# Softmax normalising on GpSimd before MLP 1, and another order and other buffers where MLP 2 follows MLP 1

## The chip, the core and the metric

One core of a Trainium2 chip runs the whole program once. The metric is the device time in microseconds (us), median of several executions. A profile of one execution gives, for each engine, every instruction with its start and its duration. Engines: PE (TensorE: matrix products, with PEld for its weight loads), DVE (VectorE), ACT (ScalarE), POOL (GpSimd) and SP (SyncE, which here issues all DMAs).

## What is computed

Windowed attention with four sink columns, then two two-layer MLPs, all in float32 at the outside:

```python
scores = where(is_sink | in_window, q @ k.T / sqrt(64), -1e9)     # 2 x 8 heads, 768 x 768, window 128
a = exp(scores - max); a = a / (a.sum(-1) + 1e-9)
x = (a @ v) -> 1536 tokens x 512
h = x @ w1_in;  g = h * clip(h + 3, 0, 6) / 6;            y = g @ w1_out      # 512 -> 2048 -> 512
h = y @ w2_in;  g = max(h, 0) + log1p(exp(-abs(h)));    out = g @ w2_out      # 512 -> 2048 -> 512
```

The kernel gets the weights as 64-bit floats. Each chunk of 128 columns or rows (512 KB) has to be turned into a high and a low part that the PE takes.

## The kernel before

**Products in three passes.** Each MLP product is three matmuls of 128x512 (high x high, high x low, low x high). An MLP step is one hidden chunk m (of 16) for one block b of 512 tokens (of 3): twelve matmuls into `h`, an activation, and twelve matmuls that add the chunk into the output (`y` in MLP 1, `o` in MLP 2).

**Attention** goes in 48 turns n of 128 queries and two heads. `e_S` makes the scores, `at_exp` (L354, L358) the masked exponentials and their sums, `at_N` (L363) normalises them, `e_T` (L433) and `e_Ts` (L447) transpose them, `e_V` multiplies by v, two turns behind. In `at_N`, L367 and L368 make the reciprocal of the sums on DVE, L371 gathers the normalised sink columns `Ps` on DVE (128x64), and L376 to L379 scale the two heads' `Pt` in place (128x288 each): head 1 on ACT, head 0 on DVE. Turns 0 to 15 come ahead of MLP 1; the other 32 are woven into MLP 1's matmuls by a list (`line`) with due times counted in matmuls.

**Weights.** `w_load` brings a chunk into one of 32 places over the SP queue; `w_conv` (L512) converts it: L28, L29, L32 on DVE, L31 and a copy on ACT (`w<-wraw`, L256), and the subtraction for the low part on POOL (`w<-wraw,w`, L253). `w_step(n)` converts up to n loaded chunks in queue order. `stand` notes a DVE instruction, and for MLP 1's chunks (`gated`, L510) the conversion's DVE instructions are put behind the last but one that was noted. A place comes free (`w_free`) when the last block's step of that chunk has read it.

**MLP 1** runs 48 steps and two more (`for s`, L785): at step s, `m1_h` and `m1_g` of step s and `m1_y` of step s - 2. Activations go through pools `rp` (tile `r`, two buffers) and `gp` (tile `G`, two). During the last block (s from 32) each step appends one or two chunks of MLP 2 to `w2` and loads one; `w_step(2)` converts. The two last steps (s = 48, 49) run `m2_h`, MLP 2's first two products. Then `st_m1` closes `rp`, `gp` and the PSUM pools, and `open_left` opens on the left side `e2` (tiles `ab`, `l`, `d`), `ps_h3` and `ps_o`.

**MLP 2** (`for s`, L821) does at step s `m2_h`, `m2_e` (ACT: L736 to L738), `m2_g` of step s - 1 (DVE L745, L747, L748; POOL `d<-ab,d`, L253; ACT and DVE for G) and `m2_o` of step s - 5. `G2` has three buffers, `h2` in PSUM three and one more.

**Order.** Score, attention and MLP 1 matmuls and the first loads stay in program order. Everything else is ordered for each engine by the framework's scheduler, by program order as priority and by when it takes its inputs to be there. Each engine then runs its queue strictly in order: an instruction that waits holds all behind it.

Of the kernel before, what the change touches and what calls it, by code (L numbers as in the profile page):

```python
# [8 lines left out]
F32 = mybir.dt.float32  # L9
BF16 = mybir.dt.bfloat16  # L10
F32R = mybir.dt.float32r
I32 = mybir.dt.int32
AF = mybir.ActivationFunctionType
ALU = mybir.AluOpType
# [4 lines left out]
SK = 32  # L19
# [158 lines left out]
def window_attention_hardswish_softplus(  # L178
# [17 lines left out]
    nc = tc.nc  # L196
# [3 lines left out]
    P = 128  # L200
    NP = H // 2
    KD = DM // P
    KF = DFF // P
# [9 lines left out]
    left = "left"  # L213
# [4 lines left out]

    TH, TS = (6, 9), 15

    NPP, NRP, NWX = 4, 2, 2

    WL0, WS0 = 1, 14

# [1 line left out]
    right = "right"  # L226
# [16 lines left out]
    T2 = 512  # L243
# [5 lines left out]
    def f32(ap):  # L249
        return ap.bitcast(F32)  # L250

    def sub(eng, out_, a, b):
        return eng.tensor_tensor(out=out_, in0=a, in1=b, op=ALU.subtract)  # L253

    def acopy(out_, in_, scale_=1.0):
        nc.scalar.activation(out=out_, in_=in_, func=AF.Copy, scale=scale_)  # L256
# [70 lines left out]
    A, M, L, pools = {}, {}, {}, {}  # L327
# [11 lines left out]
    def cols(n):  # L339
        k, i = divmod(n, 2)  # L340
        g, p, b, ib = blk(k)
        t = 2 * ib + i
        if t == 0:
            return t, 0, SK + P + SK
        if ib == 0:
            return t, SK, 2 * P + SK
        return t, i * (P + SK), 2 * P + SK
# [15 lines left out]
    def at_N(n):  # L363
        t, c0, w = cols(n)
        Pt = A["P", n]
        sm = A.pop(("sum", n))
        nc.vector.tensor_scalar(sm, sm, 1e-9, None, op0=ALU.add)  # L367
        nc.vector.reciprocal(sm, sm)  # L368
        cs = 0 if t == 0 else P
        Ps = AT["ep"].tile([P, 2, SK], F32, name="Ps", tag="Ps")  # L370
        nc.vector.tensor_tensor(out=Ps, in0=Pt[:, :, cs:cs + SK], in1=sm[:, :, None].to_broadcast([P, 2, SK]),  # L371
                                op=ALU.mult)
        A["Ps", n] = Ps

        for h in range(2):
            if h == 1 or (4 * NP <= n < 8 * NP and n % 2 == 1):  # L376
                acopy(Pt[:, h, :w], Pt[:, h, :w], sm[:, h:h + 1])
            else:
                i = nc.vector.tensor_scalar(Pt[:, h, :w], Pt[:, h, :w], sm[:, h:h + 1], None, op0=ALU.mult)  # L379
                if n < 4 * NP:  # L380
                    stand(i)

# [104 lines left out]
    wq = []  # L489
# [6 lines left out]
    def w_load(kind, m):  # L496
        tag = places.pop(0)
        w = wp.tile([P, 512, 2], I32, name="wraw", tag=tag)
        (load if kind[0] == "1" else nc.sync.dma_start)(
            w.rearrange("p (k f) t -> p k (f t)", k=KD), weight_source(kind[1], m, srcs_w[kind], P, KD))  # L500
        W["raw", kind, m] = w, tag

    after = []

    def stand(ins):
        after.append(ins.ins)
        del after[:-2]

    def gated(kind):
        return len(after) == 2 and kind[0] == "1"  # L510

    def w_conv(kind, m):  # L512

# [21 lines left out]
    def w_step(n=1):  # L535
        for _ in range(n):
            if wq and ("raw",) + wq[0] in W:
                w_conv(*wq.pop(0))
# [28 lines left out]
    def m1_g(b, m):  # L567
        r = M.pop(("r", b, m))
        G = L["gp"].tile([P, 2, T2], F32R, name="G", tag="G")
        acopy(G[:, 0], r)  # L570
        stand(sub(nc.vector, G[:, 1], r, f32(G[:, 0])))
        M["G", b, m] = G

    def m1_y(b, m):
        G = M.pop(("G", b, m))
        if m == 0:
            M["y", b] = [L["ps_y"].tile([P, T2], F32, name=f"y{d}", tag=f"y{d}") for d in range(KD)]
        w = W["1o", m]
        for d in range(KD):
            for j, (a, e) in enumerate(PASSES):  # L580
                mm(out=M["y", b][d], lhsT=w[:, a, d * P:(d + 1) * P], rhs=G[:, e, :],
                   start=(m == 0 and j == 0), stop=(m == KF - 1 and j == 2))
# [19 lines left out]
    L1, L2 = 2, 5  # L602
# [34 lines left out]
    seq = [(b, m) for b in range(NB2) for m in range(KF)]  # L637
    wq = [(kd, m) for m in range(KF) for kd in ("1i", "1o")]
# [2 lines left out]

    KE = 2 * NP
    st_m1 = ExitStack()
    L["rp"] = st_m1.enter_context(tc.tile_pool(name="rp", bufs=NRP, side=left))
    L["ps_h"] = st_m1.enter_context(tc.tile_pool(name="ps_h", bufs=NH, space=PSUM, side=left))
    st_at = e_open()
    st_ps = e_banks(4, 3)
# [35 lines left out]
            w_step()  # L683
    st_ps.close()

    L["gp"] = st_m1.enter_context(tc.tile_pool(name="gp", bufs=2, side=left))
    L["ps_y"] = st_m1.enter_context(tc.tile_pool(name="ps_y", bufs=1, space=PSUM, side=left))
    st_ps = e_banks(NS, NTV)

    n2, n3 = n1 + 4 * NP, n1 + 8 * NP  # L690
# [5 lines left out]
    seq2 = [(b, m) for b in (0, 2, 1) for m in range(KF)]  # L696
    st_m2 = ExitStack()

    def open_right():
        pools["yr"] = st_m2.enter_context(tc.tile_pool(name="yr", bufs=1, side=right))  # L700
        pools["g2"] = st_m2.enter_context(tc.tile_pool(name="g2", bufs=3, side=right))
        pools["ps_h2"] = st_m2.enter_context(tc.tile_pool(name="ps_h2", bufs=NS + NTV, space=PSUM, side=right))

    def open_left():
        pools["e2"] = st_m2.enter_context(tc.tile_pool(name="e2", bufs=2, side=left))
        pools["ps_h3"] = st_m2.enter_context(tc.tile_pool(name="ps_h3", bufs=NH, space=PSUM, side=left))
        pools["ps_o"] = st_m2.enter_context(tc.tile_pool(name="ps_o", bufs=1, space=PSUM, side=left))

# [12 lines left out]
    def m2_h(b, m):  # L721
        w_ready("2i", m)
        Y = M["Y", b]
        hp = pools["ps_h3" if m % 4 < NH and "ps_h3" in pools else "ps_h2"].tile([P, T2], F32, name="h2", tag="h2")
        w = W["2i", m].rearrange("p a (k f) -> p a k f", k=KD)
        for kk in range(KD):
            for j, (a, e) in enumerate(PASSES):
                nc.tensor.matmul(out=hp, lhsT=w[:, a, kk, :], rhs=Y[:, kk, e, :],  # L728
                                 start=(kk == 0 and j == 0), stop=(kk == KD - 1 and j == 2))
        M["h2", b, m] = hp  # L730

    def m2_e(b, m):
        hp = M["h2", b, m]
        ab = pools["e2"].tile([P, T2], F32, name="ab", tag="ab")
        l = pools["e2"].tile([P, T2], F32, name="l", tag="l")
        nc.scalar.activation(out=ab, in_=hp, func=AF.Abs)  # L736
        nc.scalar.activation(out=ab, in_=ab, func=AF.Exp, scale=-1.0)
        nc.scalar.activation(out=l, in_=ab, func=AF.Ln, bias=1.0, scale=1.0)  # L738
        M["e2", b, m] = (ab, l)

    def m2_g(b, m):
        hp, (ab, l) = M.pop(("h2", b, m)), M.pop(("e2", b, m))
        G = pools["g2"].tile([P, 2, T2], F32R, name="G2", tag="G2")
        d = pools["e2"].tile([P, T2], F32, name="d", tag="d")
        nc.vector.tensor_scalar(d, ab, 1.0, -1.0, op0=ALU.add, op1=ALU.add)  # L745
        sub(nc.gpsimd, d, ab, d)
        nc.vector.scalar_tensor_tensor(out=l, in0=hp, scalar=0.0, in1=l, op0=ALU.max, op1=ALU.add)  # L747
        nc.vector.tensor_tensor(out=l, in0=l, in1=d, op=ALU.add)  # L748
        acopy(G[:, 0], l)
        stand(sub(nc.vector, G[:, 1], l, f32(G[:, 0])))  # L750
        M["G2", b, m] = G
# [22 lines left out]
                nc.sync.dma_start(out=dst, in_=o)  # L774

    opened = False
    w2 = []

    def w2_load(n):
        for kind_m in w2[:n]:  # L780
            wq.append(kind_m)
            w_load(*kind_m)
        del w2[:n]

    for s in range(len(seq) + L1):  # L785
        cur = seq[s] if s < len(seq) else None
        prev = seq[s - L1] if s >= L1 else None
        for _ in range(2):
            if wl:
                w_load(*wl.pop(0))  # L790
        if cur:
            w_ready("1i", cur[1])
            m1_h(*cur)
        else:
            m2_h(0, s - len(seq))
        if cur:
            m1_g(*cur)
        if prev:
            w_ready("1o", prev[1])
            m1_y(*prev)  # L800
            if prev[1] == KF - 1:
                m1_yout(prev[0])
        w_step(2)
        if not line and not opened:
            opened = True
            st_ps.close()
            st_at.close()
            open_right()
            at_flag()
            y_load(0)  # L810
        for kind, bm in (("2i", cur), ("2o", prev)):
            if bm and bm[0] == NB2 - 1:
                w2.append((kind, bm[1]))
                w_free("1" + kind[1], bm[1])
        w2_load(1)
    w2_load(len(w2))
    assert opened
    st_m1.close()
    open_left()

    for s in range(len(seq2) + L2):  # L821
        if s < len(seq2):
            b, m = seq2[s]
            if s == 4:
                y_load(1)
            if s >= L1:
                m2_h(b, m)
            m2_e(b, m)
        if 1 <= s <= len(seq2):
            m2_g(*seq2[s - 1])  # L830
        w_step()
        if s >= L2:
            m2_o(*seq2[s - L2])
        w_step()
    st_m2.close()
    st_fin.close()


# [62 lines left out]
```

## Time and profile before

| | |
|---|---|
| median of 3 runs | 695.05 us (694.83 to 695.4) |
| profiled execution: device time, span | 694.55 us, 692.8 us |
| PE busy | 656.7 us, 95% |
| DVE, ACT, POOL busy | 421.7, 381.9, 151.2 us |
| granted TensorE clock, mean | 0.981 |

A busy time is the sum of an engine's instructions. A wait is the idle time of an engine ahead of an instruction, with what ended it in brackets. PE busy time is modelled: its matmuls overlap, so a step's length is better read from the starts of its groups.

### The profile page before, as it was taken

To read this page: it belongs to the slowest core of one execution; us is meant where nothing else is said; L and a number is where in the kernel's file an instruction comes from. 1 tells how busy PE (TensorE), PEld (TensorE's weight loads), DVE (VectorE), ACT (ScalarE), POOL (GpSimd) and SP (SyncE) were. 2 spreads that over 40 slices of the span, in tenths; PEclk is the share of its full clock that TensorE was granted. 3 is DMA by queue.
4 is the path that set the end of the run, shared out by engine and by line. 5 is a ranking of instruction groups with operands and counts; after the bars stand their busy time and mean duration, and the time that the engine had idled before them with its cause. 6 is when DMAs were issued, how large, how long until landed. Compare 5 with 4: busy or idle time off the path is not lost.

```text
span 692.8 us, 9020 instructions
## 1 busy us (share of the span) xinstructions
PE 656.7 (95%) x3151; PEld 493.7 (71%) x3151; DVE 421.7 (61%) x931; ACT 381.9 (55%) x783; POOL 151.2 (22%) x116
## 2 busy tenths in 40 slices
PE   7879899999999999999999996999999999999996
PEld 4446566666676777778787774888888888888884
DVE  4798988887444443425688888954445444454441
ACT  4898777776444554434545667654445444444441
POOL 0013333333000000000244444442222222222220
PEclk8998999999999999999999998999999999999999
DMA  6999652111112100004855541000001000010001
GB/s 186 258 268 294 202 164 86 32 30 48 35 50 80 40 29 16 1 12 146 267 187 180 179 145 38 1 0 1 0 1 61 0 1 1 1 61 0 1 0 66
DMA packets 39541, 54.93 MB, mean 79 GB/s; under 512 B 3136, under 2 KB 29504, under 8 KB 39232
## 3 DMA queue, kind: packets, MB, share of 16 engines
q1 hardware_dynamic: 39488, 54.28, 26.1%
q8 instruction: 27, 0.44, 0.3%
q14 instruction: 26, 0.21, 0.1%
HBM read 49.02 MB, written 5.24 MB: 78 GB/s over the span
## 4 chain that ended last, share of the span: by engine, by line
PE 64%; DVE 20%; ACT 9%; issue 3%; DMA 3%; SPq 0%; ACTq 0%; DVEq 0%
PE o L761 19%; PE h L728 18%; PE hp L263 9%; PE y L263 9%; DVE wraw L32 5%; DVE G L253 3%; PE etv L263 3%; DVE wraw L28 3%; PE s L263 3%; DVE wraw L29 3%; ACT Pt L358 2%; PE etv L433 2%; DVE r L564 2%; DMA wraw<-w_in_dram 2%; ACT wraw L31 1%
## 5 line engine op out<-in xcount | busy, mean ns | idle before, releaser
L253 POOL TENSOR_TENSOR w<-wraw,w 128x512 fp32r<-128x512 f32 x64 | 86.5, 1357 | 346.1 <-ACT w L256 344.7
L263 PE MATMUL y<-G,w 128*128 128x512 f32 x576 | 156.3, 404 | 4.6 <-DVE G L253 2.9
L761 PE MATMUL o<-w,G 128*128 128x512 f32 x576 | 139.2, 392 | 0.0
L263 PEld LDWEIGHTS y<-G,w 128*128 128x128 f32 x576 | 103.8, 189 | 30.3 <-DVE G L253 6.9
L761 PEld LDWEIGHTS o<-w,G 128*128 128x128 f32 x576 | 108.2, 188 | 23.9
L263 PE MATMUL hp<-X,w 128*128 128x512 f32 (+1 forms) x444 | 118.0, 401 | 0.3 <-DVE r L564 0.3
L253 POOL TENSOR_TENSOR d<-ab,d 128x512 f32<-128x512 f32 x48 | 64.7, 1348 | 175.6 <-DVE d L745 175.6
L263 PEld LDWEIGHTS hp<-X,w 128*128 128x128 f32 x444 | 78.7, 190 | 24.8 <-issue 9.2
L728 PE MATMUL h<-X,w 128*128 128x512 f32 x384 | 92.2, 389 | 0.0
L728 PEld LDWEIGHTS h<-X,w 128*128 128x128 f32 x384 | 72.1, 188 | 15.1
L358 ACT ACTIVATE Pt<-Pt,negm 128x288 f32<-128x288 f32 (+1 forms) x96 | 49.3, 515 | 56.7 <-DVE negm L354 55.6
L253 DVE TENSOR_TENSOR G<-l,G 128x512 fp32r<-128x512 f32 x48 | 36.0, 751 | 64.6 <-ACT G L256 64.6
L253 DVE TENSOR_TENSOR G<-r,G 128x512 fp32r<-128x512 f32 x48 | 40.8, 851 | 42.5 <-ACT G L256 42.4
L256 ACT ACTIVATE G<-l 128x512 fp32r<-128x512 f32 x48 | 30.3, 631 | 57.3 <-PE o L761 57.2
L256 ACT ACTIVATE w<-wraw 128x512 fp32r<-128x512 f32 x64 | 42.8, 679 | 33.3 <-DVE wraw L32 32.5
L31 ACT ACTIVATE wraw<-wraw 128x512 f32<-128x512 f32 x64 | 42.9, 674 | 25.8 <-DVE wraw L29 25.8
L728 PE MATMUL h<-Y,w 128*128 128x512 f32 x192 | 48.9, 406 | 6.6 <-DVE l L747 6.6
L354 DVE CUSTOM_DVE_ANT_0 Pt<-s,mask 128x288 f32<-128x288 f32 (+1 forms) x96 | 38.8, 436 | 26.3 <-PE s L263 25.9
L32 DVE SCALAR_TENSOR_TENSOR wraw<-wraw 128x512 int32<-128x512 int32 x64 | 47.8, 751 | 6.9 <-ACT wraw L31 6.1
L747 DVE SCALAR_TENSOR_TENSOR l<-h,l 128x512 f32<-128x512 f32 x48 | 33.1, 692 | 29.9 <-ACT l L738 29.8
L738 ACT ACTIVATE l<-ab 128x512 f32<-128x512 f32 x48 | 30.2, 632 | 35.8 <-DVE G L253 35.8
L728 PEld LDWEIGHTS h<-Y,w 128*128 128x128 f32 x192 | 37.2, 195 | 16.0 <-DVE l L747 7.0
(75 smaller groups left out, 754.1 us busy)
## 6 DMA issues: line engine op xcount, KB each, us to landing
wraw<-w_in_dram SPq DMA_DIRECT2D x32, 512.0 KB, 4.6
wraw<-w_out_dram SPq DMA_DIRECT2D x32, 512.0 KB, 4.8
eqk<-qk_dram SPq DMA_DIRECT2D x32, 176.0 KB, 3.6
ev<-vt_dram SPq DMA_DIRECT2D x16, 192.0 KB, 3.5
eqk<-qk_dram SPq DMA_DIRECT2D x16, 144.0 KB, 3.0
yd<-r SPq DMA_DIRECT2D x8, 256.0 KB, 2.8
yr<-yd SPq DMA_DIRECT2D x2, 1024.0 KB, 6.0
out_dram<-yr SPq DMA_DIRECT2D x2, 1024.0 KB, 4.2
```

The lines of the kernel that those rows point to most:

```text
L28: nc.vector.tensor_scalar(lo, lo, 29, None, op0=ALU.logical_shift_right)
L31: nc.scalar.activation(out=hi.bitcast(F32), in_=hi.bitcast(F32), func=AF.Copy, scale=WS)
L32: nc.vector.scalar_tensor_tensor(out=hi, in0=hi, scalar=3, in1=lo, op0=ALU.logical_shift_left, op1=ALU.bitwise_or)
L253: return eng.tensor_tensor(out=out_, in0=a, in1=b, op=ALU.subtract)
L256: nc.scalar.activation(out=out_, in_=in_, func=AF.Copy, scale=scale_)
L263: return pin(nc.tensor.matmul(**kw))
L354: nc.vector.tensor_tensor_reduce(out=Pt[:, h, :w], in0=s[:, :w], in1=masks[min(t, 2)][:, :w], scale=-scale, scalar=3.0e38, op0=ALU.add, op ...
L358: nc.scalar.activation(out=Pt[:, h, :w], in_=Pt[:, h, :w], func=AF.Exp, scale=-1.0, bias=negm[:, u:u + 1], accum_out=A["sum", n][:, h:h + 1],)
L728: nc.tensor.matmul(out=hp, lhsT=w[:, a, kk, :], rhs=Y[:, kk, e, :], start=(kk == 0 and j == 0), stop=(kk == KD - 1 and j == 2))
L738: nc.scalar.activation(out=l, in_=ab, func=AF.Ln, bias=1.0, scale=1.0)
L747: nc.vector.scalar_tensor_tensor(out=l, in0=hp, scalar=0.0, in1=l, op0=ALU.max, op1=ALU.add)
L761: nc.tensor.matmul(out=M["o", b][t], lhsT=G[:, e, t * P:(t + 1) * P], rhs=w[:, a, :], start=(m == 0 and j == 0), stop=(m == KF - 1 and j = ...
```

## The change

In turns 0 to 15 the gathering of `Ps` and the scaling of both heads' `Pt` go to GpSimd; the instruction noted by `stand` there is the reciprocal. For MLP 2's chunks, the loads go in the order in which MLP 2 needs them, one for each place that comes free, and conversions are gated as MLP 1's are; from s = 32 on, two are converted in even steps and one in odd ones, and in MLP 2 one a step instead of two. `rp` gets a third buffer. `rp` and `gp` stay open through MLP 2: `d` uses `rp`, and two of three `G` use `gp`. `e2` moves to the right side, opened when attention ends, so that `m2_e` of the first two steps and `m2_g` of the first go into steps 48 and 49.

```diff
-    NPP, NRP, NWX = 4, 2, 2
+    NPP, NRP, NWX = 4, 3, 2
...
-        nc.vector.reciprocal(sm, sm)
+        i = nc.vector.reciprocal(sm, sm)
+        if n < 4 * NP:
+            stand(i)
...
-        nc.vector.tensor_tensor(out=Ps, in0=Pt[:, :, cs:cs + SK], in1=sm[:, :, None].to_broadcast([P, 2, SK]),
-                                op=ALU.mult)
+        early = n < 4 * NP
+        (nc.gpsimd if early else nc.vector).tensor_tensor(
+            out=Ps, in0=Pt[:, :, cs:cs + SK], in1=sm[:, :, None].to_broadcast([P, 2, SK]), op=ALU.mult)
         for h in range(2):
-            if h == 1 or (4 * NP <= n < 8 * NP and n % 2 == 1):
+            if early:
+                nc.gpsimd.tensor_scalar(Pt[:, h, :w], Pt[:, h, :w], sm[:, h:h + 1], 1.0, op0=ALU.mult, op1=ALU.mult)
+            elif h == 1 or (n < 8 * NP and n % 2 == 1):
                 acopy(Pt[:, h, :w], Pt[:, h, :w], sm[:, h:h + 1])
...
     def gated(kind):
-        return len(after) == 2 and kind[0] == "1"
+        return len(after) == 2
...
-    L["rp"] = st_m1.enter_context(tc.tile_pool(name="rp", bufs=NRP, side=left))
+    st_sb = ExitStack()
+    L["rp"] = st_sb.enter_context(tc.tile_pool(name="rp", bufs=NRP, side=left))
...
-    L["gp"] = st_m1.enter_context(tc.tile_pool(name="gp", bufs=2, side=left))
+    L["gp"] = st_sb.enter_context(tc.tile_pool(name="gp", bufs=2, side=left))
...
-        pools["g2"] = st_m2.enter_context(tc.tile_pool(name="g2", bufs=3, side=right))
+        pools["g2"] = st_m2.enter_context(tc.tile_pool(name="g2", bufs=1, side=right))
+        pools["e2"] = st_m2.enter_context(tc.tile_pool(name="e2", bufs=2, side=right))
...
     def open_left():
-        pools["e2"] = st_m2.enter_context(tc.tile_pool(name="e2", bufs=2, side=left))
...
-        G = pools["g2"].tile([P, 2, T2], F32R, name="G2", tag="G2")
-        d = pools["e2"].tile([P, T2], F32, name="d", tag="d")
+        M["n2"] = M.get("n2", -1) + 1
+        G = (pools["g2"] if M["n2"] % 3 == 0 else L["gp"]).tile([P, 2, T2], F32R, name="G", tag="G")
+        d = L["rp"].tile([P, T2], F32, name="r", tag="r")
...
-    w2 = []
-
-    def w2_load(n):
-        for kind_m in w2[:n]:
-            wq.append(kind_m)
-            w_load(*kind_m)
-        del w2[:n]
+    w2 = sorted(((kd, m) for m in range(KF) for kd in ("2i", "2o")), key=lambda x: x[1] + (x[0] == "2o") * (L1 + L2))
+
+    def w2_load():
+        wq.append(w2[0])
+        w_load(*w2.pop(0))
...
             m2_h(0, s - len(seq))
+            m2_e(0, s - len(seq))
+            if s > len(seq):
+                m2_g(0, s - len(seq) - 1)
...
-        w_step(2)
+        w_step(2 if s < 2 * KF or s % 2 == 0 else 1)
...
             if bm and bm[0] == NB2 - 1:
-                w2.append((kind, bm[1]))
                 w_free("1" + kind[1], bm[1])
-        w2_load(1)
-    w2_load(len(w2))
-    assert opened
+                w2_load()
+    assert opened and not w2
...
-    for s in range(len(seq2) + L2):
+    for s in range(L1, len(seq2) + L2):
...
-            if s >= L1:
-                m2_h(b, m)
+            m2_h(b, m)
             m2_e(b, m)
-        if 1 <= s <= len(seq2):
+        if s <= len(seq2):
             m2_g(*seq2[s - 1])
         w_step()
         if s >= L2:
             m2_o(*seq2[s - L2])
-        w_step()
     st_m2.close()
+    st_sb.close()
```

## Rows read from the trace of the kernel before

**Rows 1.** Busy time by stretch: stretch, length; engines' busy us; clock, DMA share, GB/s.

```profile
10.00:41.00 31.00, 27.04 (x183) 15.39 (x184) 21.97 (x109) 26.89 (x87) 0.00 (x0) 0.89 0.93 257
41.00:61.00 20.00, 16.15 (x106) 8.94 (x103) 19.93 (x56) 17.15 (x44) 6.83 (x5) 0.83 1.08 269
61.00:175.00 114.00, 105.79 (x547) 73.51 (x547) 95.77 (x229) 85.45 (x195) 36.66 (x27) 0.99 0.35 108
...
310.00:419.00 109.00, 104.38 (x448) 82.63 (x447) 85.97 (x131) 58.85 (x98) 37.37 (x28) 1.00 0.55 179
419.00:439.00 20.00, 13.44 (x51) 10.43 (x50) 18.10 (x28) 15.15 (x29) 8.47 (x7) 0.83 0.08 26
439.00:670.00 231.00, 231.00 (x1011) 189.51 (x1010) 115.64 (x180) 109.34 (x178) 60.40 (x46) 1.00 0.03 10
```

**Rows 2.** Chain of waits, 24 to 30 us: start us, us, what.

```profile
24.78 0.74 PE s L263 x4
...
26.00 1.15 ACT Pt L358 x4
...
27.68 1.45 PE etv L263 x12
...
29.67 0.44 PE s L263
```

**Rows 3.** DVE by form (busy us, mean ns): 41 to 61; last row 10 to 41.

```profile
L371 DVE TENSOR_TENSOR Ps<-Pt,sm 128x64 f32<-128x64 f32 x4 | 3.5, 886 | 0.0
L28 DVE TENSOR_SCALAR wraw<-wraw 128x512 int32<-128x512 int32 x6 | 3.5, 591 | 0.0
...
L32 DVE SCALAR_TENSOR_TENSOR wraw<-wraw 128x512 int32<-128x512 int32 x5 | 3.3, 683 | 0.0
L379 DVE TENSOR_SCALAR Pt<-Pt,sm 128x288 f32<-128x288 f32 x5 | 1.8, 362 | 0.0
...
L371 DVE TENSOR_TENSOR Ps<-Pt,sm 128x64 f32<-128x64 f32 x13 | 2.9, 222 | 0.2
```

**Rows 4.** Timeline at 44 us, POOL and DVE: start us, us, what.

```profile
44.01 1.30 POOL L253 TENSOR_TENSOR w<-wraw,w 128x512 fp32r<-128x512 f32 x1 [43.56 <-ACT w L256]
...
44.10 1.28 DVE L371 TENSOR_TENSOR Ps<-Pt,sm 128x64 f32<-128x64 f32 x1
```

**Rows 5.** Timeline of PE, MLP 1's last block: y groups, each after an h group.

```profile
316.00 2.88 PE L263 MATMUL y<-G,w 128*128 128x512 f32 x12
...
321.44 2.88 PE L263 MATMUL y<-G,w 128*128 128x512 f32 x12
...
330.80 0.98 PE L263 MATMUL y<-G,w 128*128 128x512 f32 x3 [1.72 <-DVE r L598]
...
409.92 0.39 PE L263 MATMUL y<-G,w 128*128 128x512 f32 x1
...
415.95 0.39 PE L263 MATMUL y<-G,w 128*128 128x512 f32 x1
```

**Rows 6.** Timeline at 409 us, POOL and DVE, one step of that block.

```profile
408.59 1.32 POOL L253 TENSOR_TENSOR w<-wraw,w 128x512 fp32r<-128x512 f32 x1 [1.41 <-ACT w L256]
...
409.07 1.38 DVE L253 TENSOR_TENSOR G<-r,G 128x512 fp32r<-128x512 f32 x1 [0.40 <-ACT G L256]
```

**Rows 7.** Timeline where MLP 2 follows MLP 1, PE and ACT.

```profile
407.12 2.96 PE L728 MATMUL h<-Y,w 128*128 128x512 f32 x12
...
419.18 5.06 PE L728 MATMUL h<-Y,w 128*128 128x512 f32 x21
...
426.17 1.09 ACT L736 ACTIVATE ab<-h 128x512 f32<-128x512 f32 x2
...
430.81 1.65 PE L728 MATMUL h<-Y,w 128*128 128x512 f32 x3 [6.56 <-DVE l L747]
```

**Rows 8.** Chain of waits from 430 us.

```profile
439.11 2.76 PE o L761 x12
441.87 2.80 PE h L728 x12
```

More of the change, by code (lines that the diff above doesn't have):

```diff
@@ L367, in at_N @@
         nc.vector.tensor_scalar(sm, sm, 1e-9, None, op0=ALU.add)
-        nc.vector.reciprocal(sm, sm)
+        i = nc.vector.reciprocal(sm, sm)
+        if n < 4 * NP:
+            stand(i)
         cs = 0 if t == 0 else P
         Ps = AT["ep"].tile([P, 2, SK], F32, name="Ps", tag="Ps")
-        nc.vector.tensor_tensor(out=Ps, in0=Pt[:, :, cs:cs + SK], in1=sm[:, :, None].to_broadcast([P, 2, SK]),
-                                op=ALU.mult)
+        early = n < 4 * NP
+        (nc.gpsimd if early else nc.vector).tensor_tensor(
+            out=Ps, in0=Pt[:, :, cs:cs + SK], in1=sm[:, :, None].to_broadcast([P, 2, SK]), op=ALU.mult)
         A["Ps", n] = Ps
         for h in range(2):
-            if h == 1 or (4 * NP <= n < 8 * NP and n % 2 == 1):
+            if early:
+                nc.gpsimd.tensor_scalar(Pt[:, h, :w], Pt[:, h, :w], sm[:, h:h + 1], 1.0, op0=ALU.mult, op1=ALU.mult)
+            elif h == 1 or (n < 8 * NP and n % 2 == 1):
                 acopy(Pt[:, h, :w], Pt[:, h, :w], sm[:, h:h + 1])
             else:
-                i = nc.vector.tensor_scalar(Pt[:, h, :w], Pt[:, h, :w], sm[:, h:h + 1], None, op0=ALU.mult)
-                if n < 4 * NP:
-                    stand(i)
+                nc.vector.tensor_scalar(Pt[:, h, :w], Pt[:, h, :w], sm[:, h:h + 1], None, op0=ALU.mult)
     def e_load(k):
```

## The prediction

> **What bounds the kernel now.** I read the page first, for PE's share of the span (95%), then busy time by stretch, because that share averages stages with different limits. Six stretches are shown [rows 1]. From 439 to 670 us PE leaves no gap, so an edit there can give nothing. The rest is where PE waits: 4.0 us missing from 10 to 41, 3.9 from 41 to 61, 8.2 from 61 to 175, 4.6 from 310 to 419, 6.6 from 419 to 439. The next question is what ends last in each of them.
>
> From 10 to 41 us the first attention turns run, and the chain of waits shows a pair of turns: scores at 24.78, exponentials on ACT at 26.00, PE's product with v at 27.68, the next pair's scores at 29.67 [rows 2]. That is 4.89 us a pair, and neither the gathering of Ps nor the scaling of Pt is on it. They run beside the chain.
>
> From 41 to 61 us, the last turns ahead of MLP 1, the first five weight conversions have joined. DVE is busy for 19.93 of 20 us [rows 1]: here it is the bound. 5.3 us of this are Ps (3.5) and Pt (1.8) [rows 3]. But a part of the DVE time is no work. Ps takes 0.222 us on average ahead of this stretch and 0.886 in it [rows 3]; one Ps took 1.28 us and ended with a POOL subtraction of 1.30 that had begun 0.1 us before it [rows 4]. While POOL runs, such a DVE instruction stands still.
>
> From 316 to 416 us, MLP 1's last block with MLP 2's conversions, the length of a step is the distance of two y groups: 5.44 us at first (316.00 to 321.44) and 6.03 at the end (409.92 to 415.95) [rows 5]. There are 17 steps between the first row of the group and the last: 99.95 us, where 17 x 5.44 is 92.5. So 7.5 us are lost, 1.7 of them at one wait for a copy of y into `r`. The late steps lose theirs with two conversions each: G's subtraction on DVE takes 1.38 us beside a POOL subtraction of 1.32 that began 0.5 us earlier [rows 6], and ACT and DVE hand work to each other through queues that hold both conversions and activations.
>
> From 419 to 439 us MLP 2 follows. Its first product is done at 410 us, but ACT begins its exponential part at 426.17 [rows 7], since `e2` lies in the room that `rp` and `gp` leave only after MLP 1's last product. The fourth product needs PSUM that this part has to free: PE waits 6.56 us [rows 7], then runs at a granted clock that makes the stretch's mean 0.83 [rows 1]. From 419.18 to the first `o` at 439.11 four products are run, each 2.80 at full clock [rows 7, 8]: 19.9 us for 11.2, so 8.7 are lost.
>
> **The change, part by part.** All sums are made against the profiled execution, 694.55 us (its span 692.8 and 1.75 around it), 0.5 below the median; I carry differences over to the median, 695.05.
>
> A. *Ps and Pt on GpSimd, turns 0 to 15.* DVE loses the 5.3 us above from 41 to 61, and ACT its five scalings of head 1 there. From 10 to 41 nothing is gained, as the chain doesn't hold them. POOL gets 64 + 2 x 288 columns a turn. The trace has no scaling on POOL; its nearest row is 1.30 us for 512 columns of two inputs [rows 4]. Taken by columns, that is 1.63 us a turn, under the 2.45 of a turn. From above, all three instructions cost 1.30 each, 3.9 a turn; from below they cost what is hidden, nothing. I take 1.63, since columns should count. It lies on the way to the transposes two turns later, and what slack there is comes from that distance. From 41 to 61 POOL then has 6.8 + 4 x 1.63 = 13.3 us, and what DVE's conversions have there is 3.5 + 3.4 + 3.3 = 10.2 (L28, L32 and, like L32, L29) [rows 1, 3]. If the two can't overlap at all they need 23.5 us, so the stretch grows by 3.5; if DVE's own work is the bound it shrinks by 5.3. I take -2, with both ends kept. The loads run at a DMA share of 1.08 there [rows 1], which also speaks against the full 5.3. The changed `stand` moves only where conversions may begin: 0.
>
> The page SBUF — State Buffer of the Trainium skill, section Who interferes with whom, says that GpSimd and a DVE instruction with two SBUF inputs, or in a two-port mode, exclude each other for the whole instruction. The 1.28 us of rows 4 agree with it. By that rule part A gives +3.5 and not -2; it is the first rival below.
>
> B. *1.5 conversions a step, order of need, gating, a third `r`.* Half a conversion a step less is about 1 us of DVE (L28 0.59, L29 and L32 0.68 each [rows 3]) and a third of a POOL lock, against a loss of 0.59 a late step. So late steps should come near 5.44. The third `r` takes the 1.72 us wait on a copy of y away, if no other wait follows. Gating puts a conversion's DVE instructions behind an older G subtraction; what is queued behind them are the next r and G, and PE's y waits for these two steps later, so there is cover of some 8 us. Each load still waits on the SP queue for its place, ahead of y's stores and the reload of y; one late chunk costs DVE up to a load of some us, and that keeps the end at 0. Ends -7.5 and 0; I take -4.5.
>
> C. *`e2`, `d` and G in room that is free early; m2_e and m2_g in the last steps.* ACT can take the first product at 410 us, so the PSUM of the fourth is free long before PE gets there. Both the 6.56 us wait and the slow clock after it go. What is late next is DVE: 18.10 us of work from 419 to 439 [rows 1], some of it the copies of y, which may now lie elsewhere. Ends -8.7 and 0; I take -7.5.
>
> D. *Eight conversions put off into MLP 2, one a step.* DVE has 115.64 us of work in 231 us there [rows 1], 2.75 in a step of 5.5; a conversion adds some 2.0. PE covers it, 0; without that cover it would be up to eight times the excess over 5.5, which is none. G keeps three places in all: 0.
>
> Sum: -2 - 4.5 - 7.5 = -14.0, so 681.0 us.
>
> **Rivals.**
> 1. *The lock.* POOL's scaling and DVE's conversions exclude each other from 41 to 61, A is +3.5: 695.05 + 3.5 - 12 = 686.5. For it speaks that DVE's busy time there holds such waits already; against it that the scaling of early turns can be done before 41.
> 2. *DVE takes the place of the wait.* The 18.10 us from 419 to 439 stay and PE needs 11.2, so 6.9 of the 8.7 stay: C is -1.8, and the time 686.7. Against it: step 48's part begins 16 us earlier, and the block before has DVE idle for a fifth.
> 3. *Slower: GpSimd is the bound ahead of MLP 1.* At 3.9 us a turn, 16 turns and five subtractions are 62.4 + 6.8 = 69.2 us on POOL where 51 are there (10 to 61): +18.2, less 12, so 701.2. It decides from (51 + 12 - 6.8) / 16 = 3.5 us a turn on. The nearest row speaks for half of that.
> 4. *It does not do what it says.* The scheduler sorts loads and conversions anyway, and places what is moved where it was: 695.
>
> **How the numbers follow.** Chances: the forecast 0.54, with a range of its own from 676 to 686; rival 1 0.18, rival 2 0.12, rival 3 0.08, rival 4 0.05; all good ends together (-21.5, 673.5) 0.03. A range from 674 to 691 holds the forecast, rivals 1 and 2 and a mix of both with some loss in B, over 0.8. A difference under 0.2%, 1.4 us, can't be told from none here. Faster: 0.54 + 0.18 + 0.12 + 0.03 = 0.87; same 0.05; slower 0.08.
>
> **What the profile after would show.** A right: first matmuls of MLP 1 begin some 2 us before 61, POOL scalings near 0.7 us, and DVE rows of Ps gone; wrong if DVE's conversions there have means well over 0.7 us or PE waits for POOL. B right: y groups 5.44 apart up to the last. C right: no wait over 1 us between MLP 1's last y and MLP 2's first o, at a clock of 1.0. The prediction is wrong if POOL's scaling costs over 1.3 us, or if a new wait of several us stands at the junction, on DVE or for a load.

## The result, and the profile after

The changed kernel takes 688.25 us (median of 4 runs, 687.97 to 688.9) against 695.14 for the kernel before in the same comparison: a ratio of 0.990 (95% interval 0.9885 to 0.9919), or -6.9 us. The forecast was 681.0. The sign and the range of 674 to 691 held; the size was half of what was forecast.

The profiled execution has a span of 686.0 us, against 692.8. Its busy time by stretch, in the columns of [rows 1] and for the same stretches:

```profile
10.00:41.00 31.00, 26.08 (x178) 14.89 (x178) 16.35 (x81) 21.81 (x73) 15.21 (x36) 0.89 0.94 257
41.00:61.00 20.00, 14.74 (x93) 8.22 (x92) 19.13 (x53) 16.30 (x43) 15.62 (x17) 0.83 1.05 255
61.00:175.00 114.00, 104.92 (x559) 72.58 (x560) 94.72 (x228) 85.03 (x195) 36.63 (x27) 1.00 0.36 111
310.00:419.00 109.00, 106.19 (x465) 86.02 (x465) 80.31 (x117) 55.18 (x92) 31.62 (x24) 1.00 0.57 184
419.00:439.00 20.00, 17.44 (x73) 13.22 (x73) 17.44 (x27) 14.72 (x27) 9.00 (x7) 1.00 0.00 1
439.00:670.00 231.00, 230.07 (x1003) 187.90 (x1004) 131.20 (x199) 115.31 (x189) 69.60 (x51) 1.00 0.03 10
```

Against [rows 1], DVE lost 5.6 us of work from 10 to 41 us, where nothing waited for it, but only 0.8 from 41 to 61, where it is the bound. PE gained 1.8 us from 310 to 419 and 4.0 from 419 to 439, at full clock. The last line is new in kind: 15.6 us more DVE work in MLP 2.

To place the 6.8 us, compare starts of PE's groups: MLP 1's first product, the `y` groups of [rows 5], the first `o` groups. After:

```profile
63.50 1.21 PE L263 MATMUL hp<-X,w 128*128 128x256 f32 x8
...
316.90 2.88 PE L263 MATMUL y<-G,w 128*128 128x512 f32 x12
322.34 2.88 PE L263 MATMUL y<-G,w 128*128 128x512 f32 x12
...
406.32 2.79 PE L263 MATMUL y<-G,w 128*128 128x512 f32 x11 [0.86 <-DVE G L253]
...
411.75 0.39 PE L263 MATMUL y<-G,w 128*128 128x512 f32 x1
...
418.92 5.87 PE L732 MATMUL h<-Y,w 128*128 128x512 f32 x24 [0.66 <-DVE l L753]
425.47 3.06 PE L732 MATMUL h<-Y,w 128*128 128x512 f32 x12 [0.68 <-DVE l L753]
...
428.37 2.93 PE L767 MATMUL o<-w,G 128*128 128x512 f32 x12
434.45 2.92 PE L767 MATMUL o<-w,G 128*128 128x512 f32 x12
441.90 2.92 PE L767 MATMUL o<-w,G 128*128 128x512 f32 x12
447.46 2.96 PE L767 MATMUL o<-w,G 128*128 128x512 f32 x12
```

Two groups of the kernel before that [rows 5, 8] don't hold in this form:

```profile
61.13 1.69 PE L263 MATMUL hp<-X,w 128*128 128x256 f32 x12
...
438.94 2.93 PE L761 MATMUL o<-w,G 128*128 128x512 f32 x12
```

| place | before | after | difference | forecast |
|---|---|---|---|---|
| start of the last block (first `y` shown) | 316.00 | 316.90 | +0.9 | A: -2 |
| from there to its last `y` | 99.95 | 94.85 | -5.1 | B: -4.5 |
| from the last `y` to the first `o` | 22.99 | 16.62 | -6.4 | C: -7.5 |
| from the first `o` to the end of the span | 253.86 | 257.63 | +3.8 | D: 0 |
| span | 692.8 | 686.0 | -6.8 | -14 |

B and C came out within about 1 us. The 7 us that are missing lie in A (+0.9 for -2) and D (+3.8 for 0). The 2.4 us by which MLP 1's first product is late have shrunk to 1.0 at 175 us, up to which PE has gaps [rows 1], and to 0.9 at the last block. Not all of this 0.9 need be A's: that block starts at 316.3 to 317.2 us in the traces of the seven kernels with the whole of A, and at 315.8 to 316.6 in five without it, 0.7 apart on average.

### The profile page after: what moved, and what is told of

Its sections match the earlier page's. It is cut to its first block, busy times and chain, and to the rows that moved or that the text cites. A ratio compares the mean times of both kernels' runs of the same rounds, so it can differ in the third digit from the quotient of the medians.

```text
span 686.0 us, 9046 instructions
## 1 busy us (share of the span) xinstructions
PE 651.7 (95%) x3151; PEld 490.9 (72%) x3151; DVE 420.2 (61%) x899; ACT 374.7 (55%) x767; POOL 177.9 (26%) x164
## 5 line engine op out<-in xcount | busy, mean ns | idle before, releaser
L253 POOL TENSOR_TENSOR w<-wraw,w 128x512 fp32r<-128x512 f32 x64 | 90.7, 1427 | 300.3 <-ACT w L256 285.6
L263 PE MATMUL y<-G,w 128*128 128x512 f32 x576 | 153.2, 400 | 2.1 <-DVE G L253 2.1
L253 POOL TENSOR_TENSOR r<-ab,r 128x512 f32<-128x512 f32 x48 | 64.8, 1350 | 159.3 <-DVE r L751 158.9
L253 DVE TENSOR_TENSOR G<-r,G 128x512 fp32r<-128x512 f32 x48 | 45.3, 945 | 57.0 <-ACT G L256 56.8
L354 DVE CUSTOM_DVE_ANT_0 Pt<-s,mask 128x288 f32<-128x288 f32 (+1 forms) x96 | 38.6, 436 | 30.3 <-PE s L263 28.6
L732 PEld LDWEIGHTS h<-Y,w 128*128 128x128 f32 x192 | 35.5, 188 | 13.9 <-DVE l L753 5.8
```

The source lines that it names most:

```text
L263: return pin(nc.tensor.matmul(**kw))
L354: nc.vector.tensor_tensor_reduce(out=Pt[:, h, :w], in0=s[:, :w], in1=masks[min(t, 2)][:, :w], scale=-scale, scalar=3.0e38, op0=ALU.add, op ...
```

## Experiments

Each edit is on the kernel before or on the changed one, as said. Medians stand beside the ratio to the kernel before, with its interval; the kernel before had medians of 695.1 to 696.0 in these comparisons. A span and group starts are of the profiled execution.

### D: what do the conversions put off into MLP 2 cost?

**A conversion every second step** (changed kernel):

```diff
-        w_step()
+        if s % 2 == 0:
+            w_step()
         if s >= L2:
             m2_o(*seq2[s - L2])
```

> The kernel after with MLP 2's eight deferred conversions one every second step instead of one a step. If what slows MLP 2's first steps (6.1 to 7.5 us between two o groups, 3.9 in all) is that a conversion a step makes DVE, with its waits for GpSimd, the bound, half as many leave room: these steps go to 5.5 to 5.6 and the time to 684 to 685.5. Rival, the buffers that d and G now share, or the gating, slow them: they stay over 6 us, 688.

684.32 us, 0.985 (0.9825 to 0.9878). The span is 682.5. PE's `o` groups in it:

```profile
428.76 2.92 PE L767 MATMUL o<-w,G 128*128 128x512 f32 x12
435.10 2.92 PE L767 MATMUL o<-w,G 128*128 128x512 f32 x12
440.67 2.90 PE L767 MATMUL o<-w,G 128*128 128x512 f32 x12
446.21 2.96 PE L767 MATMUL o<-w,G 128*128 128x512 f32 x12
```

From the first `o` to the end are 253.7 us, as before the change (253.9). After one long step (6.34) the steps are 5.54 to 5.6, where the changed kernel has 6.08, 7.45 and, further on, 6.16, 6.54 and 6.23. In either kernel seven conversions begin behind the first `o`, so it is their rate, not their number.

How this comes about in the changed kernel, by DVE's groups from 428 to 473 us (busy us, mean ns of one, then idle time ahead) and by the timeline of one long step:

```profile
L28 DVE TENSOR_SCALAR wraw<-wraw 128x512 int32<-128x512 int32 x7 | 9.2, 1314 | 0.0
L253 DVE TENSOR_TENSOR G<-l,G 128x512 fp32r<-128x512 f32 x7 | 7.6, 1091 | 2.1 <-ACT G L256 2.1
L32 DVE SCALAR_TENSOR_TENSOR wraw<-wraw 128x512 int32<-128x512 int32 x7 | 5.9, 840 | 0.6
L29 DVE SCALAR_TENSOR_TENSOR wraw<-wraw 128x512 int32<-128x512 int32 x7 | 5.3, 763 | 0.1
...
L253 DVE TENSOR_TENSOR X<-yr,X 128x512 fp32r<-128x512 f32 x4 | 2.7, 684 | 0.0
```

```profile
436.53 1.53 POOL L253 TENSOR_TENSOR w<-wraw,w 128x512 fp32r<-128x512 f32 x1 [2.77 <-issue]
436.82 1.53 DVE L751 TENSOR_SCALAR r<-ab 128x512 f32<-128x512 f32 x1
...
438.27 0.68 DVE L753 SCALAR_TENSOR_TENSOR l<-h,l 128x512 f32<-128x512 f32 x1
...
439.00 3.06 PE L732 MATMUL h<-Y,w 128*128 128x512 f32 x12 [1.63 <-DVE l L753]
```

Two things were not in the sum. A conversion takes DVE 1.31 + 0.76 + 0.84 = 2.9 us here, not the 2.0 taken, and G's subtraction 1.09, because POOL now has two subtractions in each step (`r<-ab,r` and `w`) and DVE stands still beside both. And the copies `X<-yr` for the next block, 0.68 us each, come in just these steps. DVE is busy for 41.0 of 45 us, and its queue is in order: at 436.82 an instruction that takes 0.42 us alone takes 1.53 beside POOL; behind it stands `l`, which frees the PSUM for PE's next product, and PE waits 1.63 us.

**C alone** (kernel before, with the pools, `m2_e` and `m2_g` of the change; two conversions a step, so all are done before MLP 2):

```diff
-        pools["g2"] = st_m2.enter_context(tc.tile_pool(name="g2", bufs=3, side=right))
+        pools["g2"] = st_m2.enter_context(tc.tile_pool(name="g2", bufs=1, side=right))
+        pools["e2"] = st_m2.enter_context(tc.tile_pool(name="e2", bufs=2, side=right))
...
             m2_h(0, s - len(seq))
+            m2_e(0, s - len(seq))
+            if s > len(seq):
+                m2_g(0, s - len(seq) - 1)
```

> The kernel before with part C alone (e2 on the right side, d and G in rp and gp, m2_e and m2_g in steps 48 and 49); loads, conversions and gating as before. If C takes the whole wait ahead of MLP 2's first o and the deferred conversions are what slows MLP 2's first steps in the kernel after, then the late steps of MLP 1's last block stay at 6.0 us, the stretch to the first o shrinks by 6.4 to 8.7, MLP 2's steps stay near 5.5 and the time is 686.5 to 689. Rival, DVE takes the place of the wait by itself: MLP 2's first steps are over 6 us here too and the time is 690 to 693.

686.61 us, 0.9886 (0.987 to 0.9903): no worse than the whole change, and as expected if the put-off conversions are what slows MLP 2. Its last `y` starts at 415.82 and its first `o` at 431.55, 15.73 us where 22.99 were: -7.3. From there to the end of its span (684.7) are 253.15 us, so MLP 2 loses nothing. Steps of the last block still end at 6.05 to 6.35. Its busy time in the last 13 us before MLP 2's first `o` shows what the junction is bound by then:

```profile
419.00:432.00 13.00, 11.96 (x51) 9.29 (x51) 12.27 (x18) 10.40 (x20) 6.15 (x5) 1.00 0.13 40
```

DVE is busy for 94% of it; PE has lost 1 us, at full clock.

**Gating of MLP 1's chunks only** (changed kernel):

```diff
-        return len(after) == 2
+        return len(after) == 2 and kind[0] == "1"
```

> The kernel after with gating for MLP 1's chunks alone, as before. If gating keeps DVE from standing at a load that hasn't landed, MLP 1's last block gets a step of 7 us or more again, 689 to 691. If it only shifts conversions against GpSimd's subtractions, late steps and MLP 2's first steps change by some tenths either way: 686.5 to 689.

686.50 us, 0.9877 (0.9861 to 0.9894). The scheduler moves the conversions forward again, and only one begins behind the first `o`: the late steps of the block are 6.03 to 6.38 as before the change, and the first `o` comes at 431.40, with 5.74 and 5.56 to the next two. So without the gate the loss goes back from MLP 2 to the block. The time is 1.8 us shorter, with intervals that overlap: what the gate wins in the block it loses again in MLP 2. The 7.49 us step stays away, so the gate isn't what removed it.

### B: which part of it carries the gain?

**Two conversions in every step** (changed kernel):

```diff
-        w_step(2 if s < 2 * KF or s % 2 == 0 else 1)
+        w_step(2)
```

> The kernel after with two conversions in every step of MLP 1's last block, so that none is left for MLP 2. If the number of conversions a step sets the step's length, late steps go back from 5.44 to about 6.0 (some 5 us lost) and MLP 2's first steps go to 5.5 (some 4 us won): 688 to 690. Rival, the order of need and the gating gave the shorter steps and the number didn't: late steps stay at 5.44 and the time is 684 to 685.

698.58 us, 1.0051 (1.0034 to 1.0068): slower than the kernel before, which neither expectation had. Late steps are 7.05 us long (389.68, 396.74, 403.80). One of them:

```profile
399.55 1.40 POOL L253 TENSOR_TENSOR w<-wraw,w 128x512 fp32r<-128x512 f32 x1 [2.00 <-ACT w L256]
399.69 1.55 DVE L28 TENSOR_SCALAR wraw<-wraw 128x512 int32<-128x512 int32 x1
```

In this order the first conversion's L28, at 398.62, takes 0.42 us, and the second's begins just behind a POOL subtraction and takes 1.55; G's subtraction at 396.72 takes 1.38, and PE waits 0.91 us for it in each of these steps. Without the gate two conversions a step made steps of 6.05 to 6.35 (C alone). That the gate makes this order is read from these traces and not tested by itself. It shortens the block's steps only with fewer conversions a step.

**A third `r` alone taken back** (changed kernel, `NRP` 2), and **C with a third `r`** (C alone, `NRP` 3):

```diff
-    NPP, NRP, NWX = 4, 3, 2
+    NPP, NRP, NWX = 4, 2, 2
```

> The kernel after with two buffers of r. If the third buffer took away the step of 7.5 us (a copy of y that waits for a store), it is back and the time is some 2 us longer, 690. Rival, the gating or the order took it away: 688.2.

> The kernel before with part C and a third buffer of r, nothing else. If the third buffer alone takes away the step of 7.5 us in MLP 1's last block: 2 us under part C alone (686.6), 684.6. Rival, a conversion that stands at its load is the cause and the buffer doesn't matter: 686.6.

Without it 691.59 us, 0.9956 (0.9939 to 0.9972), and the wait of [rows 5] is back:

```profile
331.12 0.96 PE L263 MATMUL y<-G,w 128*128 128x512 f32 x3 [1.71 <-DVE r L601]
```

C with it takes 685.17 us, 0.9872 (0.9845 to 0.9898), and the step of 7.49 us becomes one of 5.44. The step gives 2.05 us, with no other wait after it. The medians say 1.4 (beside C alone, with intervals that overlap) and 3.3 (in the changed kernel, whose MLP 2 takes 257.7 us with two `r` as with three); neither is better known than that.

**A nearer order of need** (changed kernel):

```diff
-    w2 = sorted(((kd, m) for m in range(KF) for kd in ("2i", "2o")), key=lambda x: x[1] + (x[0] == "2o") * (L1 + L2))
+    w2 = sorted(((kd, m) for m in range(KF) for kd in ("2i", "2o")), key=lambda x: x[1] + (x[0] == "2o") * L1)
```

> The changed kernel with MLP 2's chunks loaded and converted in a nearer order (the out chunks sorted two steps behind the in chunks and not seven). If the new order of need carries part B, steps near the last block's end grow or MLP 2's first steps wait for in chunks more: over 690. If the gain of B comes from 1.5 conversions a step and the third r alone, the time stays at 687.5 to 689.

687.81 us, 0.9894 (0.9873 to 0.9915), no difference from the changed kernel. This much of the order carries nothing; the kernel before's own order wasn't put into the changed one.

### A: why does GpSimd not help?

**A alone** (kernel before) and **all but A** (changed kernel). The edit is the change's in `at_N`, with the reciprocal as noted instruction, once put in and once left out:

```diff
+        early = n < 4 * NP
+        (nc.gpsimd if early else nc.vector).tensor_tensor(
+            out=Ps, in0=Pt[:, :, cs:cs + SK], in1=sm[:, :, None].to_broadcast([P, 2, SK]), op=ALU.mult)
...
+            if early:
+                nc.gpsimd.tensor_scalar(Pt[:, h, :w], Pt[:, h, :w], sm[:, h:h + 1], 1.0, op0=ALU.mult, op1=ALU.mult)
```

> The kernel before with part A alone (Ps and both heads' Pt on GpSimd in turns 0 to 15). In the trace after, MLP 1's first product began at 63.5 us, 2.4 us later than before, and 1.5 of that was gone by 310 us. If GpSimd's hold on the SBUF port shared with DVE is the cost, the first product is again 2 to 3 us late and the time is 0.5 to 2.4 us longer than before: 695.5 to 697.5. Rival, A relieves DVE and the delay came from another part: first product at 61 or sooner, 693 to 695.

> The kernel after with part A undone and all else kept. If A costs what its shift at 310 us shows, 0.9 us: 687.3, with the first product at 61.1. Rival, A pays (DVE relief is worth more further on): 689 to 690.

A alone takes 696.33 us, 1.0016 (1.0007 to 1.0026), with MLP 1's first product at 63.49; all but A takes 688.21, 0.9904 (0.9887 to 0.992), with that product at 61.37. A costs 2.1 to 2.4 us there. At the end it costs 1.1 us in the kernel before and nothing in the changed one (688.21 for 688.25): neither the expected 687.3 came nor the rival's 689 to 690.

GpSimd isn't the bound. Its groups in the changed kernel, 10 to 41 us and then 41 to 61:

```profile
L380 POOL TENSOR_SCALAR Pt<-Pt,sm 128x288 f32<-128x288 f32 x16 | 8.4, 539 | 0.8
L375 POOL TENSOR_TENSOR Ps<-Pt,sm 128x64 f32<-128x64 f32 x12 | 3.5, 294 | 23.7 <-DVE sm L368 14.9 <-ACT EPT L256 5.5 <-ACT EPTs L256 2.5
```

```profile
L253 POOL TENSOR_TENSOR w<-wraw,w 128x512 fp32r<-128x512 f32 x5 | 8.4, 1681 | 0.0
L380 POOL TENSOR_SCALAR Pt<-Pt,sm 128x288 f32<-128x288 f32 x8 | 6.2, 782 | 0.4
```

A turn takes 0.29 + 2 x 0.54 = 1.4 us ahead of 41 us, under the 1.63 that I took. Among the conversions the scaling grows to 0.78 and the subtraction to 1.68; in the kernel before, its five there took 6.83 us [rows 1], 1.37 each.

**A for turns 0 to 11**, so that turns 12 to 15, beside which the conversions run, stay on DVE and ACT; and **Ps alone** on GpSimd (both on the kernel before; first the line in which 12 turns differ from A alone, then Ps alone):

```diff
+        early = n < 12
...
-        nc.vector.tensor_tensor(out=Ps, in0=Pt[:, :, cs:cs + SK], in1=sm[:, :, None].to_broadcast([P, 2, SK]),
-                                op=ALU.mult)
+        (nc.gpsimd if n < 4 * NP else nc.vector).tensor_tensor(
+            out=Ps, in0=Pt[:, :, cs:cs + SK], in1=sm[:, :, None].to_broadcast([P, 2, SK]), op=ALU.mult)
```

> The kernel before with part A for turns 0 to 11 only; turns 12 to 15, beside which the weight conversions run (41 to 61 us), keep Ps and Pt on DVE and ACT. Part A alone delayed MLP 1's first product by 2.4 us (61.1 to 63.5). If that is the exclusion between GpSimd and DVE among the conversions, the delay goes: first product at 61 to 62, time 695 to 695.7. If it is the early turns, whose pair grew from 4.89 to 5.0 us as the exponentials' DVE step now also waits for GpSimd, the delay stays mostly: 62.5 to 63.5, time 696 to 696.5.

> The kernel before with only the gathering of Ps (0.29 us on GpSimd) moved for turns 0 to 15; the scaling of Pt and the noted instruction stay. If DVE's 3.5 us of Ps between 41 and 61 us were work that can be got rid of, the first product comes 1 to 3 us earlier, at 58 to 60, time 692 to 694. If DVE's time there is mostly standing still beside GpSimd, which moves to the next DVE instruction, the first product stays at 60.7 to 61.7 and the time at 694.5 to 695.7.

A for 12 turns: 697.91 us, 1.0051 (1.0028 to 1.0074), first product at 63.73. So scalings beside the conversions aren't needed for the delay. Ps alone: 697.75 us (693.69 to 698.83), 1.0033 (1.0008 to 1.0057), first product at 62.09. Both are slower than expected in either case. From 41 to 61 us, where Ps had 0.886 us a piece [rows 3], these DVE groups stand still most: in the changed kernel (two lines), with 12 turns, and with Ps alone (the last line is a wait):

```profile
L32 DVE SCALAR_TENSOR_TENSOR wraw<-wraw 128x512 int32<-128x512 int32 x7 | 5.8, 828 | 0.4 <-ACT wraw L31 0.4
L367 DVE TENSOR_SCALAR sm<-sm 128x2 f32<-128x2 f32 x5 | 3.3, 655 | 0.7 <-ACT Pt L358 0.7
...
L29 DVE SCALAR_TENSOR_TENSOR wraw<-wraw 128x512 int32<-128x512 int32 x6 | 6.2, 1055 | 0.0
...
L29 DVE SCALAR_TENSOR_TENSOR wraw<-wraw 128x512 int32<-128x512 int32 x6 | 5.1, 845 | 0.0
...
L379 DVE TENSOR_SCALAR Pt<-Pt,sm 128x288 f32<-128x288 f32 x5 | 1.8, 368 | 2.2 <-POOL Ps L371 2.0
```

The 3.5 us of Ps were mostly standing still beside POOL. Take Ps away, and another instruction stands still: L367 on two columns goes from 0.391 us in the kernel before to 0.655, L29 from 0.683 to 1.055 with 12 turns and 0.845 with Ps alone. With Ps alone there is a new wait as well: the scaling (L379) writes the tile from which POOL gathers Ps, and DVE sits idle for 2.0 us until POOL is done with it.

**The noted instruction alone** (kernel before, nothing on GpSimd), and **A for turns 0 to 7** with the old noted instruction:

```diff
-        nc.vector.reciprocal(sm, sm)
+        i = nc.vector.reciprocal(sm, sm)
+        if n < 4 * NP:
+            stand(i)
```

> The kernel before with only the noted instruction changed, from the scaling of Pt to the reciprocal; nothing goes to GpSimd. Part A alone delayed MLP 1's first product by 2.4 us, and between 37 and 46 us, where its first conversions run, the attention turns fell 1.6 us behind: 13 conversion steps of DVE begin there up to 46 us, against 6 before. If the earlier note is what lets them in, this kernel does the same without GpSimd: first product at 62 to 63, and conversions from 37.5 to 38.2 on; time 695 to 696. If GpSimd's work is the cause (the early end of scaling on DVE leaves it the room), the first product stays at 60.8 to 61.6.

> The kernel before with Ps and Pt of turns 0 to 7 on GpSimd, the rest and the noted instruction as before. If the early turns carry a loss of their own (pairs of 5.0 to 5.2 us in place of 4.7 to 5.1), the turns are 0.5 to 0.9 us late at 37 us and the first product is at 61.6 to 62.2. If all of the loss is made by the conversions' place, the first product stays at 60.8 to 61.5 and the time at 694.5 to 695.7.

The noted instruction alone: 694.71 us, 0.999 (0.9981 to 0.9999), and the first product at 59.85, 1.3 us earlier. It isn't the cause; it helps a little. A for 8 turns: 698.26 us, 1.0037 (1.0023 to 1.0051), first product at 62.73, later than either expectation. The early turns carry a loss of their own. The time doesn't follow the first product in these runs: 8 turns, 12 turns and Ps alone have medians over that of A alone, with executions that differ by 2 to 5 us, and what makes this isn't known. In the kernel with 8 turns, POOL and the first step of the exponentials:

```profile
19.11 0.29 POOL L372 TENSOR_TENSOR Ps<-Pt,sm 128x64 f32<-128x64 f32 x1
19.50 0.83 POOL L378 TENSOR_SCALAR Pt<-Pt,sm 128x192 f32<-128x192 f32 x2
20.41 0.46 DVE L354 CUSTOM_DVE_ANT_0 Pt<-s,mask 128x288 f32<-128x288 f32 x1 [0.92 <-POOL Pt L378]
```

L354 of turn 5 begins 0.08 us after POOL's scaling of turn 4 ends at 20.33, having waited 0.92 us. Of this 0.5 us are lost: its scores begin at 19.08, and in the kernel before L354 begins 0.79 us after its scores do where DVE is idle (34.71 and 35.50, turn 11). It isn't the standing still of [rows 4], for elsewhere L354 begins and runs its 0.45 us in the midst of POOL's scalings (at 42.68 us of the changed kernel, beside a pair from 42.08 to 43.62). L354 writes `Pt`, which POOL now scales, and it is on the chain that sets the turns' time. With four buffers the `Pt` that it writes was scaled four turns earlier; why it follows this newest scaling isn't settled.

How much this makes is seen from L354 of turn 4 to that of turn 12, ahead of most conversions. The timeline of the kernel before, and of A for 8 turns:

```profile
17.80 0.36 DVE L354 CUSTOM_DVE_ANT_0 Pt<-s,mask 128x192 f32<-128x192 f32 x1 [0.91 <-PE s L263]
...
37.17 0.17 DVE L367 TENSOR_SCALAR sm<-sm 128x2 f32<-128x2 f32 x1 [0.83 <-ACT Pt L358]
37.25 0.45 DVE L354 CUSTOM_DVE_ANT_0 Pt<-s,mask 128x288 f32<-128x288 f32 x1
```

```profile
17.07 0.36 DVE L354 CUSTOM_DVE_ANT_0 Pt<-s,mask 128x192 f32<-128x192 f32 x1 [1.02 <-PE s L263]
...
37.36 0.17 DVE L367 TENSOR_SCALAR sm<-sm 128x2 f32<-128x2 f32 x1 [0.84 <-ACT Pt L358]
37.56 0.17 DVE L368 RECIPROCAL sm<-sm 128x2 f32<-128x2 f32 x1
37.76 0.22 DVE L372 TENSOR_TENSOR Ps<-Pt,sm 128x64 f32<-128x64 f32 x1
37.91 0.45 DVE L354 CUSTOM_DVE_ANT_0 Pt<-s,mask 128x288 f32<-128x288 f32 x1
```

That is 19.45 us and 20.84. In the same way the changed kernel takes 20.85, A alone 20.6 and A for 12 turns 20.6; all but A takes 19.9 and the noted instruction alone 19.3. Over the traces of all runs it is 20.6 to 21.2 us with scalings on GpSimd and 19.3 to 19.9 with none of A's work there. In the changed kernel these 1.4 us, and 0.9 more up to the first product, make the 2.4 us of delay.

L354's wait for POOL is only a part of the 1.4. From turn 4 to 5 the traces with A take 0.4 us more on average (3.0 to 3.7 us against 2.7 to 3.3). From turn 11 to 12 they take 0.5 more (2.2 to 2.3 us against 1.75 to 1.76 in each without), and there L354 waits for nothing on POOL: DVE's queue has another order. Before, it stands right behind L367; with 8 turns behind the reciprocal and Ps of turn 11 too, and in the changed kernel behind the reciprocal and the first conversion's L28, 0.60 us after L367. The scheduler has sorted DVE's queue anew where instructions left it; no run fixes the old order, so that this costs the 0.5 is read from the traces alone.

### Both failed terms undone

Changed kernel without A and with a conversion every second step; then the same with the reciprocal as noted instruction:

```diff
-        w_step()
+        if s % 2 == 0:
+            w_step()
...
-            if early:
-                nc.gpsimd.tensor_scalar(Pt[:, h, :w], Pt[:, h, :w], sm[:, h:h + 1], 1.0, op0=ALU.mult, op1=ALU.mult)
```

> The changed kernel without part A and with MLP 2's put-off conversions one in every second step. Both undone parts add up, if the reading is right: MLP 2's 231 us come back (230.8), and the first product is at 61.4 instead of 63.5, of which up to 1 us is left at the last block. Time 683.3 to 684.3. If part A helps the later parts in a way not seen so far, it is over 685.

> The changed kernel with Ps and Pt back on DVE and ACT, the reciprocal still the noted instruction, and MLP 2's put-off conversions one in every second step. If the early note alone brings MLP 1's first product forward and GpSimd's part gives it away, the first product is at 60 to 60.6 (spread without A: 61.5) and the time 682.5 to 684. If the gain ahead of MLP 1 is given back later, as it was in the kernel before with the early note alone (a first product 1.3 us earlier, 0.6 us in the time), the time is 683.5 to 684.3.

684.13 us, 0.9843 (0.9825 to 0.9861), with the first product at 61.52; and 683.98 us, 0.9832 (0.9814 to 0.9849), with it at 60.70 and a span of 682.3. Both beat both kernels by 4 us and more, but they aren't better than the changed kernel with spread conversions (684.32): what is won ahead of MLP 1 doesn't reach the end. C with a third `r` and nothing else had 685.17, with an interval that touches theirs: all the rest of the change brings some 1 us beyond these two parts at best, and costs 3 us as it was made.

## Why the prediction was half right

**C, right.** The 6.56 us wait and the low clock after it are gone [rows 7], and 0.66 and 0.68 us stand there now; C alone gives -7.3 and the whole change -6.4, for -7.5 forecast. What was named as late next, DVE, is late: it is busy for 17.44 of 20 us, and its `G` and `l` end the waits of 0.53, 0.66 and 0.68 us that stay. Rival 2 (-1.8 there) did not come at the junction; its mechanism, DVE as the next bound, came in MLP 2's first steps, under D.

**B, right in size, with a cause more.** -5.1 for -4.5. The third `r` is 2 us of it, as its row said. Late steps are 5.44 up to the last three (6.49, 5.52 and 6.67), of which the first and the third have a wait of PE for G, 0.76 and 0.86 us. What lies ahead of the second wait:

```profile
403.10 2.62 POOL L253 TENSOR_TENSOR w<-wraw,w 128x512 fp32r<-128x512 f32 x2 [4.30 <-ACT w L256]
...
404.59 1.68 DVE L253 TENSOR_TENSOR G<-r,G 128x512 fp32r<-128x512 f32 x1 [1.32 <-ACT G L256]
```

Two POOL subtractions come in a row, and G's subtraction on DVE stands still beside the second. The rest of B's gain, 3 us, is not a gain of the whole: the conversions that the block is rid of are those that cost 3.8 us in MLP 2, under D. And with two conversions in a step, gated, steps are 7.05.

**D, the step that failed most: +3.8 for 0.** "PE covers it, 0" rested on 2.75 + 2.0 = 4.75 us of DVE work in a step of 5.5. Both terms were means of the whole stretch or of another one. The first eight steps have `X<-yr` beside; DVE's durations grow when POOL has two subtractions a step. Measured from 428 to 473 us it is 41.0 of 45 us, with an in-order queue that leaves no place for what PE needs next. With half the rate the loss is gone (253.7 us for 257.6). I had the lock in hand for A and didn't ask for it here.

**A, mis-sized and of the wrong sign: 0 to +1 at the end for -2.** The row of 1.28 us beside 1.30 [rows 4] was read rightly as standing still, and then counted as work that leaves with Ps, so that "DVE loses the 5.3 us". It doesn't leave: DVE's busy time from 41 to 61 fell by 0.8 us, not 5.3. What the Trainium skill says in SBUF — State Buffer, Who interferes with whom, that GpSimd and a two-input or two-port DVE instruction exclude each other, fits these rows: in the changed kernel L367, on two columns, takes 1.26 us at 57.07 beside two POOL subtractions (3.51 us from 56.58 on). But rival 1 (+3.5 by the lock from 41 to 61) isn't what happened either: 1.4 of the 2.4 us arise ahead of turn 12, where I had written that the scaling isn't on the chain. It came onto the chain in part through the wait of L354 for POOL (some 0.4 us) and, as far as the traces show, through the new order of DVE's queue (0.5); the rest is in small pieces. The prediction followed the moved scaling to the transposes that read the tile, and not to its next writer or to what stays in DVE's queue.

**Rival 3, wrong price.** GpSimd's three instructions cost 1.4 us a turn, far from 3.5.

By place, the whole difference of 7 us to the forecast is thus D's 3.8, A's 2.9 and C's 1.1, less B's 0.6. By experiment D's 3.9 holds (684.32 for 688.25). Of A's 2.9, the 2 that were forecast as gain are missing; that A costs 0.9 at the end isn't shown, since without it the time was the same (688.21).

## What to carry to other kernels

Work put off into a stretch where an engine is half idle on average must be set against the first steps of that stretch, with durations as they are beside the other engines' work there; its rate counts, not its sum. Busy time that is really standing still beside another engine goes to the next instruction in the queue when its holder is moved, so it isn't to be booked as a gain. When a step goes to another engine, ask also for the next writer of its buffer: that one gets a new wait, as L379 did with Ps alone, and it may be on the chain when the step was not. And ask what the scheduler makes of the queue that the step has left.

## What was not expected of the hardware

A DVE instruction on 128x2 (L367) stands still beside GpSimd as one on 128x512 does: 0.655 us on average from 41 to 61 us of the changed kernel, 0.19 from 10 to 41. L354, which reads PSUM, doesn't: 0.451 and 0.455. And POOL loses too: with scalings on GpSimd its subtractions of 128x512 took 1.68 us on average from 41 to 61, in place of 1.37. The scalings aren't all of the reason, for a single one took 1.80 us (at 47.38, A for 8 turns) where POOL had no scaling left to do.
